# Linear attention and MLP layers on one core: the second value product in the sums' banks, a query product ahead of the first broadcasts, row statistics on ScalarE with spread transposes

## The chip, the cores and the metric

One Trainium2 chip, one of its cores. The metric is device time in microseconds (us) of one execution of the whole kernel; lower is better. PE is the matrix engine (TensorE), ACT the scalar engine, DVE the vector engine, POOL the GpSimd engine, SP the engine that issues the DMA transfers here. Each engine works through its own instructions in order and waits for the others by semaphores.

## What is computed

Four residual layers run one after the other on 2048 rows of 576 features in bfloat16: linear attention (A), MLP (B), and both again with the same weights. There are 32 heads of 18 features; the MLP is 4608 wide.

```python
def _A_ref(x, wqkv, wo):
    qkv = (x @ wqkv).reshape(B, S, 3, H, Dh).transpose(2, 0, 3, 1, 4)
    q, k, v = qkv[0], qkv[1], qkv[2]
    phi = lambda t: jnp.where(t > 0, t + 1, jnp.exp(t)) + 1e-6
    pq, pk = phi(q), phi(k)
    kv = jnp.einsum("bhsd,bhse->bhde", pk, v)
    z = jnp.einsum("bhsd->bhd", pk)
    num = jnp.einsum("bhqd,bhde->bhqe", pq, kv)
    den = jnp.einsum("bhqd,bhd->bhq", pq, z)[..., None] + 1e-6
    return (num / den).transpose(0, 2, 1, 3).reshape(B, S, D) @ wo

def _B_ref(x, w1, b1, w2, b2):
    h = _gelu(_layernorm(x) @ w1 + b1)
    return h @ w2 + b2

x = x + _A_ref(_layernorm(x), wqkv, wo)
x = x + _B_ref(_layernorm(x), w1, b1, w2, b2)
x = x + _A_ref(_layernorm(x), wqkv, wo)
x = x + _B_ref(_layernorm(x), w1, b1, w2, b2)
```

## The kernel before

**Tiling.** The rows are 16 tiles of 128 (t), or 4 blocks of 512 (c). The 32 heads form 5 groups (g) of 7, 7, 7, 7 and 4 heads, so 126 or 72 columns. The normalized rows stand turned in `yT`, features on partitions.

**PSUM.** There are eight banks. `ps_h` has four one-bank buffers in rotation, which serve key and query products, transposes (`tp`), denominators and broadcasts. `ps_acc` has two buffers of two banks, accA and accB. During the keys of an A layer accA holds `kvacc`, the running sums of keys times values, and accB every value product `v_ps`.

**LayerNorm pipe.** `LNPipe` carries tiles through stages, one per `tick`: statistics (L296 to L309, DVE), the reciprocal root by a power on POOL (L315), `ln_nmr` (L319), the norm into one of three `y_ring` buffers (L330 on POOL, L334 on DVE), and in the last stage five transposes on PE (L352) and a copy into `yT` (L354). `l0_norm_eng` (L759) gives the engine of the norm in the first layer. Other rows are turned through DRAM (`turn_rows`, `land`) and do not use PE.

**A layer, keys.** For each tile t: key product (`k_proj`, 10 matmuls, L449), a tick of the LayerNorm pipe, value product in two halves (`v_proj`, L462 and L470, copied to `v_ring` by ACT and DVE), the sums of the tile before (`kv_acc`, L488), and from some tile on one query product (`q_proj`, L494). In the first layer's opening the first value product is copied out by three ACT copies, one of them between its halves (L464 to L478). `phi` takes an exponent (L388) and a shift (L389) on ACT and two steps on DVE.

**A layer, passage.** The sums are masked (`kvT`, L518), the denominators of blocks 0 and 1 are formed and inverted (`den_stage` L556 to L564), spread (`quad_stage`, L569) and broadcast to the heads' columns by a matmul (`scale_stage`, L578), copied by ACT (L580) and multiplied into `pq` by DVE (L581). Five products `kvwo` (L540) alternate between accB and accA; odd ones are copied out by DVE (L545), even ones by ACT (L547). Four query products are woven in between.

**A layer, output.** `wo_stage` for each tile: ten matmuls (L589) into accA or accB in turn, the residual sum on DVE (L427), a store to DRAM. Between them stand the broadcasts of the next block, in the first layer the last query products, the denominators of blocks 2 and 3, and one tick of the LayerNorm pipe per tile, through which the first four tiles of the MLP (its first block) go. Each of these four is fed after its sum with `hold=1`, statistics on DVE, norm on POOL, transposes on PE, copy on ACT.

**MLP.** For each block 36 slices of the first product with GELU on ACT (L690 to L699), then the second product (L744).

PE's instructions have the order of the program text (`pe` chains them); the order on the other engines is that of a scheduler, held by the manual dependences in the text.

Of the kernel before, what the change touches and what calls it, by code (L numbers as in the profile page):

```python
# [34 lines left out]
def build(tc, A_x, A_wqkv, A_wo, B_w1, B_b1, B_w2, B_b2, out, dbg=None, n_layers=4):  # L35
    nc = tc.nc
    dbg = dbg or {}
    with ExitStack() as ctx:
# [182 lines left out]
        state = dict(ycnt=0, vcnt=0, turns=0)  # L221
# [42 lines left out]
        class LNPipe:  # L264
# [3 lines left out]
            def feed(self, xt, t, kind, norm_eng, evac_eng="dve", load_from=None, after=None, hold=0):  # L268
                self.items.append(dict(stage=(0 if load_from is None else -1), xt=xt, t=t, kind=kind,
                                       norm=norm_eng, evac=evac_eng, load=load_from,  # L270
                                       after=after, hold=hold))
# [4 lines left out]
            def tick(self, transposes=1):  # L276
                land()
                for it in list(self.items):
                    st = it["stage"]
                    if st == 4 and it["evac"] != "dma":  # L280
                        if transposes == 0:
                            continue
                        transposes -= 1
# [3 lines left out]
                    if st == -1:  # L287
# [4 lines left out]
                        it["xt"] = xn  # L292
                    elif st == 0:
# [23 lines left out]
                    elif st == 2 and it["norm"] != "dve":  # L317
                        nmr = work.tile([P, 1], F32, name="ln_nmr", bufs=4)
                        nc.gpsimd.tensor_scalar(out=nmr[:], in0=it["mv"][:, 0:1], scalar1=-1.0,  # L319
                                                scalar2=it["rstd"][:, 0:1], op0=ALU.mult, op1=ALU.mult)  # L320
                        it["nmr"] = nmr
                    elif st in (2, 3):
                        y = y_ring[state["ycnt"] % NY]
# [18 lines left out]
                    elif st == 4:  # L342
# [10 lines left out]
                        if it["evac"] == "act":  # L353
                            nc.scalar.copy(out=yT[:, :, t * P:(t + 1) * P], in_=tp)  # L354
                        else:
                            nc.vector.tensor_copy(out=yT[:, :, t * P:(t + 1) * P], in_=tp)
# [80 lines left out]
        def layer_A(li, next_kind, pre_a1=None):  # L437
            kvacc = ps_acc.tile([P, 2, 512], F32, name="kvacc", tag="accA")
# [17 lines left out]
            def v_proj(t):  # L456
# [3 lines left out]
                vp = ps_acc.tile([P, 2, 512], F32, name="v_ps", tag="accB")  # L460
# [3 lines left out]
                begin = li == 0 and t == 0  # L464
                if begin:
                    early = nc.scalar.copy(out=va[:, 0:2, 0:126], in_=vp[:, 0, 0:252].rearrange("p (g c) -> p g c", g=2))
                    for keys in ("exp", "phi"):
                        tc.add_manual_dep(early.ins, act_last[keys], NOSYNC, reason="keys before values")
                for k in range(KD):
                    pe(nc.tensor.matmul(vp[:, 1, 0:324], lhsT=yT[:, k, tok], rhs=wqkv_sb[:, k, 2 * D + 252: 3 * D],  # L470
                                     start=(k == 0), stop=(k == KD - 1)))
                if begin:
                    nc.scalar.copy(out=va[:, 2:4, 0:126], in_=vp[:, 1, 0:252].rearrange("p (g c) -> p g c", g=2))
                else:
                    nc.scalar.copy(out=va[:, 0:4, 0:126].rearrange("p (b g) c -> p b g c", b=2),
                                   in_=vp[:, :, 0:252].rearrange("p b (g c) -> p b g c", g=2))
                if begin:
# [5 lines left out]
            def kv_acc(t):  # L483
                pk = pk_tiles.pop(t)
                va = v_tiles.pop(t)
                for g in range(G):
# [30 lines left out]

            nc.vector.tensor_tensor(  # L518
# [65 lines left out]
            def wo_stage(t):  # L584
# [8 lines left out]
                if xn is not None and next_kind == "B" and t < TPC:  # L593
                    lnp.feed(xn, t, "B", "pool", "act", after="sum", hold=1)
# [22 lines left out]
            for t in range(NT):  # L617
# [141 lines left out]
        def l0_norm_eng(t):  # L759
            return "dve" if t < 2 else "pool"  # L760
# [99 lines left out]
```

## Time and profile before

| | us |
|---|---|
| median of three runs | 777.58 (777.58 to 777.61) |
| the profiled execution | 777.09 |
| its span, first to last instruction | 775.4 |
| PE busy in it | 765.1 |
| ACT busy | 335.1 |
| DVE busy | 277.7 |
| POOL busy | 120.5 |

The profile is one execution. A row of its timeline gives the start in us from the span's beginning, the length, the engine, the line, the operation with output and inputs, and how many were merged (x5); in brackets stands the time for which the engine had nothing to do before, and what ended it. A matmul's length reaches to its modelled end, later than the start of the next. Groups (`x144 | 91.2, 684 | ...`) give the count, the busy time in us, and the mean length in ns.

| stretch | us |
|---|---|
| keys of the first A layer | 7 to 67 |
| its passage | 67 to 80.5 |
| its output stage | 80.5 to 110 |
| first MLP | 110 to 395 |
| keys of the second A layer up to 449, passage | 449 to 461 |
| its output stage | 461 to 490 |
| second MLP | 490 to 775.4 |

### The profile page before, as it was taken

What the parts mean: (1) busy time and instruction counts of PE and PEld (TensorE: products, weight loads), DVE (VectorE), ACT (ScalarE), POOL (GpSimd) and SP (SyncE); (2) the same over time, 40 slices, a digit from 0 to 9 for tenths busy, and PEclk for the clock granted to TensorE, in tenths of its full rate; (3) what the DMA queues carried; (4) which work ended last, traced back from release to release, by engine and by line L of the source; (5) the groups of instructions that cost most, each with busy time, mean ns of one, the idle gap of its engine ahead of it and who ended that gap; (6) DMA issues with size and microseconds to landing.
All of it is one profiled execution on the core that took longest, in us unless ns stands there. A gap on an engine that the chain in (4) does not pass through costs nothing.

```text
span 775.4 us, 15774 instructions
## 1 busy us (share of the span) xinstructions
PE 765.1 (99%) x6613; PEld 495.0 (64%) x6613; DVE 277.7 (36%) x714; ACT 335.1 (43%) x734; POOL 120.5 (16%) x185
## 2 busy tenths in 40 slices
PE   8999999999999999999999999999999999999998
PEld 5776664675477457646777766547745764675476
DVE  7786964046013503401355579520140032000000
ACT  5888646404610650264046675561065026305600
POOL 4671322012000301200100004110030011001000
PEclk9999999999999999999999999999999999999999
DMA  8991474016301810320440006630141033011000
GB/s 254 267 299 46 137 253 103 18 50 173 88 16 48 199 50 32 92 64 17 138 107 1 1 2 210 248 82 8 32 129 52 16 124 80 8 32 54 1 11 21
DMA packets 73761, 69.10 MB, mean 89 GB/s; under 512 B 34266, under 2 KB 58330, under 8 KB 73690
## 3 DMA queue, kind: packets, MB, share of 16 engines
q1 hardware_dynamic: 73690, 68.10, 30.0%
q8 instruction: 51, 0.84, 0.5%
q14 instruction: 20, 0.16, 0.1%
HBM read 45.67 MB, written 22.41 MB: 88 GB/s over the span
## 4 chain that ended last, share of the span: by engine, by line
PE 94%; DVE 4%; issue 1%; ACT 1%; DMA 0%; POOL 0%; DVEq 0%; ACTq 0%
PE m_ps L744 37%; PE h_ps L694 20%; PE hp_ps L694 16%; PE q_ps L494 5%; PE k_ps L449 5%; PE wo_ps L589 4%; PE v_ps L470 3%; PE v_ps L462 2%; PE kvacc L488 1%; PE tp L352 1%; PE rden_ps L578 1%; PE warm_ps L176 1%; DVE rden L564 1%; DVE xo L427 0%; DMA x_d<-xo 0%
## 5 line engine op out<-in xcount | busy, mean ns | idle before, releaser
L744 PE MATMUL m_ps<-w_sb,hT 128*128 128x288 bf16 x2304 | 283.6, 286 | 0.0
L744 PEld LDWEIGHTS <-hT 128*128 128x128 bf16 x2304 | 224.8, 98 | 59.8 <-issue 3.4
L694 PEld LDWEIGHTS <-w_sb 64*128 64x128 bf16 x2304 | 124.5, 94 | 136.5 <-issue 1.9
L694 PE MATMUL hp_ps<-yT,w_sb 64*128 64x512 bf16 x1152 | 178.0, 376 | 0.0
L694 PE MATMUL h_ps<-yT,w_sb 64*128 64x512 bf16 x1152 | 148.0, 376 | 0.0
L699 ACT COPY relay_sb<-relay_sb 128x1 f32<-128x1 f32 x144 | 28.6, 198 | 264.5 <-PE h_ps L694 222.2
L315 POOL TENSOR_TENSOR ln_rstd<-ln_u,neg_half 128x1 f32<-128x1 f32 x64 | 36.8, 577 | 480.4 <-DVE ln_u L306 239.7
L690 ACT ACTIVATE hT<-h_ps,b1T 128x512 bf16<-128x512 f32 x144 | 91.2, 684 | 44.4 <-PE h_ps L694 44.4
L690 ACT ACTIVATE hT<-hp_ps,b1T 128x512 bf16<-128x512 f32 x144 | 91.2, 693 | 0.0
L427 DVE TENSOR_TENSOR xbf<-m_ps,xo 128x576 bf16<-128x576 f32 (+1 forms) x17 | 12.2, 722 | 219.9 <-PE m_ps L744 219.9
L427 DVE TENSOR_TENSOR xo<-m_ps,xo 128x576 f32<-128x576 f32 x16 | 12.1, 758 | 179.2 <-PE m_ps L744 179.2
L411 POOL TENSOR_TENSOR xo<-xo,b_bc 128x576 f32<-128x576 f32 x32 | 40.9, 1284 | 102.5 <-DMA xo<-x_d 62.7
L694 PE MATMUL h_ps<-yT,w_tail 64*128 64x512 bf16 x144 | 54.1, 376 | 0.0
L694 PE MATMUL hp_ps<-yT,w_tail 64*128 64x512 bf16 x144 | 54.1, 376 | 0.0
L494 PE MATMUL q_ps<-yT,wqkv_sb 128*126 128x512 bf16 (+1 forms) x200 | 50.0, 382 | 0.0
L589 PE MATMUL wo_ps<-kvwo,pq 126*128 126x288 bf16 (+1 forms) x320 | 43.9, 285 | 1.7 <-DVE pq L581 0.7
L449 PE MATMUL k_ps<-wqkv_sb,yT 128*128 128x288 bf16 x320 | 44.3, 286 | 0.0
L589 PEld LDWEIGHTS <-pq 126*128 126x128 bf16 (+1 forms) x320 | 30.2, 97 | 13.1 <-DVE pq L581 1.8
L449 PEld LDWEIGHTS <-yT 128*128 128x128 bf16 x320 | 31.0, 98 | 11.4
L694 PEld LDWEIGHTS <-w_tail 64*128 64x128 bf16 x288 | 27.1, 94 | 17.1
L388 ACT ACTIVATE phi_e<-k_ps 128x288 bf16<-128x288 f32 x46 | 19.3, 419 | 34.6 <-PE k_ps L449 33.6
L391 DVE TENSOR_SCALAR phi_e<-phi_e 128x288 bf16<-128x288 bf16 (+2 forms) x86 | 25.1, 292 | 24.6 <-ACT phi_e L388 24.5
(100 smaller groups left out, 633.2 us busy)
## 6 DMA issues: line engine op xcount, KB each, us to landing
xo<-x_d SPq DMA_DIRECT2D x48, 288.0 KB, 3.6
x_d<-xo SPq DMA_DIRECT2D x32, 288.0 KB, 2.1
xl<-x_d SPq DMA_DIRECT2D x24, 288.0 KB, 4.6
y_d<-turned SPq DMA_DIRECT2D x40, 144.0 KB, 3.2
w_sb<-in_B_w_dram SPq DMA_DIRECT2D x6, 864.0 KB, 9.5
yT<-y_d SPq DMA_DIRECT2D x10, 512.0 KB, 4.1
w_sb<-in_B_w_dram SPq DMA_DIRECT2D x9, 512.0 KB, 5.6
x_d<-xn SPq DMA_DIRECT2D x16, 288.0 KB, 2.2
```

The lines of the kernel that those rows point to most:

```text
L315: nc.gpsimd.tensor_tensor(out=rstd[:], in0=it["u"][:], in1=neg_half[:], op=ALU.pow)
L391: nc.vector.tensor_scalar(out=e[0:rows, 0:n], in0=e[0:rows, 0:n], scalar1=1.0, scalar2=1e-6, op0=ALU.min, op1=ALU.add)
L411: nc.gpsimd.tensor_tensor(out=xo[:], in0=xo[:], in1=b2_bc[:], op=ALU.add)
L427: total = nc.vector.tensor_tensor(out=xn[:, cols].rearrange("p (h n) -> p h n", h=nh), in0=ps, in1=xo[:, cols].rearrange("p (h n) -> p h n ...
L449: pe(nc.tensor.matmul(kp[:, 0:HALF], lhsT=yT[:, k, tok], rhs=wqkv_sb[:, k, D + half * HALF: D + (half + 1) * HALF], start=(k == 0), stop=( ...
L470: pe(nc.tensor.matmul(vp[:, 1, 0:324], lhsT=yT[:, k, tok], rhs=wqkv_sb[:, k, 2 * D + 252: 3 * D], start=(k == 0), stop=(k == KD - 1)))
L494: pe(nc.tensor.matmul(qp[0:GR[g], :], lhsT=wqkv_sb[:, k, GO[g]:GO[g] + GR[g]], rhs=yT[:, k, c * CA:(c + 1) * CA], start=(k == 0), stop=(k ...
L589: pe(nc.tensor.matmul(wp[:, half, 0:HALF], lhsT=pq[(g, c)][0:GR[g], j * P:(j + 1) * P], rhs=kvwo[g][0:GR[g], half * HALF:(half + 1) * HALF ...
L690: act_last["gelu"] = nc.scalar.activation(out=to, in_=ps, func=ACT.Gelu_apprx_tanh, bias=b1T[:, f:f + 1], scale=1.0).ins.name
L694: mm = pe(nc.tensor.matmul(dst[n], lhsT=wt, rhs=mv, start=(seen[n] == 0), stop=(seen[n] == 8)))
L699: relay = nc.scalar.copy(out=relay_sb[:, 1:2], in_=relay_sb[:, 0:1])
L744: pe(nc.tensor.matmul(acc[:, half, 0:HALF], lhsT=hT[f][:, j * P:(j + 1) * P], rhs=w2_sb[:, f, half * HALF:(half + 1) * HALF], start=(f == ...
```

## The change

It has three parts. First, in the first layer the value product of tile 1 goes into accA and `kvacc` is allocated only with the first sums; the sums of tile 0 move behind the key product of tile 2; the three ACT copies of value product 0 become one of ACT and one of DVE, and value product 1 takes the ACT copies; tile 3's norm moves from POOL to DVE. Second, in the passage of both A layers one query product moves from between `kvwo` 2 and 3 to before the first broadcasts. Third, for the four tiles that an A layer hands to the MLP, the statistics are made by two passes on ACT (an Identity with scale -1/D that sums to the negative mean, and a Square with that as its bias that sums to the variance times D), with one small step on POOL for the variance plus epsilon; no more than three tiles may hold a `y_ring` buffer; a second tick without transposes is made per output tile up to t = 9; the transposes of tile t wait until output tile 6 + 2t.

```diff
-        state = dict(ycnt=0, vcnt=0, turns=0)
+        state = dict(wo=0, ycnt=0, vcnt=0, turns=0)
...
-            def feed(self, xt, t, kind, norm_eng, evac_eng="dve", load_from=None, after=None, hold=0):
+            def feed(self, xt, t, kind, norm_eng, evac_eng="dve", load_from=None, after=None, hold=0, stats="dve", tp_at=0):
...
-                        if transposes == 0:
+                        if transposes == 0 or state["wo"] < it["tp_at"]:
                             continue
...
+                    elif st == 0 and it["stats"] == "act":
+                        mv = it["mv"] = work.tile([P, 2], F32, name="ln_mv", bufs=6)
+                        it["dump"] = blk.tile([P, D], BF16, name="ln_dump", tag="blk")
+                        nc.scalar.activation(out=it["dump"][:], in_=it["xt"][:, 0:D], func=ACT.Identity,
+                                             scale=-1.0 / D, accum_out=mv[:, 0:1])
+                        it["stage"] = 0.5
+                        continue
+                    elif st == 0.5:
+                        u = it["u"] = work.tile([P, 1], F32, name="ln_u", bufs=4)
+                        mv = it["mv"]
+                        nc.scalar.activation(out=it.pop("dump")[:], in_=it["xt"][:, 0:D], func=ACT.Square,
+                                             bias=mv[:, 0:1], accum_out=mv[:, 1:2])
+                        nc.gpsimd.tensor_scalar(out=u[:], in0=mv[:, 1:2], scalar1=(1.0 + EPS) / D, scalar2=EPS * EPS,
+                                                op0=ALU.mult, op1=ALU.add)
+                        it["stage"] = 1
+                        continue
...
+                        if sum(other["stage"] == 4 for other in self.items) == NY:
+                            continue
...
-                            nc.scalar.copy(out=yT[:, :, t * P:(t + 1) * P], in_=tp)
+                            turned_tile = nc.scalar.copy(out=yT[:, :, t * P:(t + 1) * P], in_=tp)
+                            if act_last["exp"] is not None:
+                                tc.add_manual_dep(turned_tile.ins, act_last["exp"], NOSYNC, reason="keys go on first")
...
-            kvacc = ps_acc.tile([P, 2, 512], F32, name="kvacc", tag="accA")
+            kvacc_of = {}
...
-                vp = ps_acc.tile([P, 2, 512], F32, name="v_ps", tag="accB")
+                begin = li == 0 and t < 2
+                vp = ps_acc.tile([P, 2, 512], F32, name="v_ps", tag="accA" if begin and t == 1 else "accB")
...
+                copy = nc.scalar.copy(out=va[:, 0:4, 0:126].rearrange("p (b g) c -> p b g c", b=2),
+                                      in_=vp[:, :, 0:252].rearrange("p b (g c) -> p b g c", g=2))
                 if begin:
...
+                    for keys in ("exp", "phi"):
+                        tc.add_manual_dep(copy.ins, act_last[keys], NOSYNC, reason="keys before values")
+                if begin and t == 1:
                     nc.scalar.copy(out=va[:, 4, 0:72], in_=vp[:, 1, 252:324])
                 else:
                     nc.vector.tensor_copy(out=va[:, 4, 0:72], in_=vp[:, 1, 252:324])
...
+                if t == 0:
+                    kvacc_of["ps"] = ps_acc.tile([P, 2, 512], F32, name="kvacc", tag="accA")
+                kvacc = kvacc_of["ps"]
...
+                if li == 0 and t == 2:
+                    kv_acc(0)
                 pre_a1(t)
                 v_proj(t)
-                if t >= 1:
+                if t >= (2 if li == 0 else 1):
                     kv_acc(t - 1)
...
-                    lnp.feed(xn, t, "B", "pool", "act", after="sum", hold=1)
+                    lnp.feed(xn, t, "B", "pool", "act", hold=1, stats="act", tp_at=6 + 2 * t)
...
             q_proj(*q_left.pop(0))
             kv_wo(1)
+            q_proj(*q_left.pop(0))
             for g in range(3):
                 scale_stage(g, 0)
             kv_wo(2)
-            q_proj(*q_left.pop(0))
             kv_wo(3)
...
+                state["wo"] = t
                 lnp.tick()
+                if t < 10:
+                    lnp.tick(transposes=0)
...
-            return "dve" if t < 2 else "pool"
+            return "pool" if t == 2 or t > 3 else "dve"
```

More of the change, by code (lines that the diff above doesn't have):

```diff
@@ L318, in tick @@
                         nmr = work.tile([P, 1], F32, name="ln_nmr", bufs=4)
-                        nc.gpsimd.tensor_scalar(out=nmr[:], in0=it["mv"][:, 0:1], scalar1=-1.0,
+                        nc.gpsimd.tensor_scalar(out=nmr[:], in0=it["mv"][:, 0:1], scalar1=1.0 if it["stats"] == "act" else -1.0,
                                                 scalar2=it["rstd"][:, 0:1], op0=ALU.mult, op1=ALU.mult)
@@ L463, in v_proj @@
                                      start=(k == 0), stop=(k == KD - 1)))
[L464 to L468, printed above, removed]
                 for k in range(KD):
@@ L516, in layer_A @@
             q_proj(*q_left.pop(0))
+            kvacc = kvacc_of["ps"]
             nc.vector.tensor_tensor(
```

7 lines of the change are left out of this document (1 added, 6 removed).

## The prediction

> **What bounds the kernel now.** I read the page's busy times first, then the busy time by stage, then the list of waits, and last the order of time around each wait.
>
> ```profile
> span 775.4 us, 15774 instructions
> PE 765.1 (99%) x6613; PEld 495.0 (64%) x6613; DVE 277.7 (36%) x714; ACT 335.1 (43%) x734; POOL 120.5 (16%) x185
> ```
>
> TensorE (PE) sets the end. The change neither adds nor removes a matmul, so all it can move is PE's idle time, 775.4 - 765.1 = 10.3 us by the record. The stages say where that lies:
>
> ```profile
> 7.00:15.00 8.00, 7.09 (x65) 5.50 (x63) 5.71 (x21) 5.03 (x14) 3.86 (x7) 1.00 1.06 335
> 15.00:67.00 52.00, 52.00 (x456) 40.36 (x455) 39.40 (x133) 42.70 (x104) 32.67 (x57) 1.00 0.86 246
> 67.00:80.50 13.50, 12.61 (x117) 7.92 (x116) 10.45 (x30) 11.13 (x23) 0.00 (x0) 1.00 0.01 1
> 80.50:110.00 29.50, 28.53 (x257) 19.66 (x258) 25.03 (x60) 15.79 (x28) 9.53 (x16) 1.00 0.56 192
> 449.00:461.00 12.00, 11.30 (x112) 7.10 (x109) 9.08 (x26) 9.72 (x19) 0.00 (x0) 1.00 0.00 0
> 461.00:490.00 29.00, 27.21 (x249) 18.62 (x249) 24.43 (x57) 14.58 (x26) 9.32 (x16) 1.00 0.59 200
> ```
>
> The columns are stretch, length, then PE, weight loads, DVE, ACT, POOL. PE idles 0.91 us in the opening, 0.89 and 0.70 us in the two passages from keys to the output stage, 0.97 and 1.79 us in the two output stages: 5.26 us, and all three parts of the change lie there. In the output stages DVE is the fullest of the other engines (25.03 of 29.5 us), ACT half empty. The granted clock is 1.00 in all of them. The record hides some idle time: a matmul's row runs on after the next could have started, so each stop loses about 0.16 us more than it shows (in the rows below, 0.70 against 0.54 from start to start).
>
> Two lines of the list of waits (waiting, waited for, us in total, times, longest) that the rows further down do not show:
>
> ```profile
> PE rden_ps L578 <- DVE rden L564: 0.8, 2, 0.4
> ...
> PE tp L352 <- POOL y_ring L330: 0.4, 1, 0.4
> ```
>
> **Part 1, the second value product in accA (gain 1.25 us).** The PE rows of the opening are: first half and second half of value product 0, transposes of tile 2, value product 1, sums 0, key product 2; the others are the steps that part 1 leans on.
>
> ```profile
> 4.79 1.07 POOL L315 TENSOR_TENSOR ln_rstd<-ln_u,neg_half 128x1 f32<-128x1 f32 x2 [2.49 <-DVE ln_u L306]
> ...
> 5.38 0.94 DVE L334 TENSOR_SCALAR y_ring<-x,ln_mv,ln_rstd 128x576 bf16<-128x576 bf16 x2 [0.30 <-POOL ln_rstd L315]
> ...
> 9.74 0.70 PE L462 MATMUL v_ps<-wqkv_sb,yT 128*128 128x252 bf16 x5
> ...
> 11.06 0.85 PE L470 MATMUL v_ps<-wqkv_sb,yT 128*128 128x324 bf16 x5 [0.61 <-ACT v_ring L466]
> ...
> 11.74 0.44 PE L352 MATMUL tp<-ident,y_ring 128*128 128x128 bf16 x5
> ...
> 12.32 0.71 ACT L354 COPY yT<-tp 128x640 bf16<-128x640 bf16 x1
> 12.48 0.70 PE L462 MATMUL v_ps<-wqkv_sb,yT 128*128 128x252 bf16 x5 [0.30 <-ACT v_ring L478]
> ...
> 12.52 0.15 DVE L306 TENSOR_SCALAR ln_u<-ln_mv 128x1 f32<-128x1 f32 x1
> ...
> 13.02 0.85 PE L470 MATMUL v_ps<-wqkv_sb,yT 128*128 128x324 bf16 x5
> ...
> 13.71 0.42 PE L488 MATMUL kvacc<-pk,v_ring 128*128 128x126 bf16 x5
> ...
> 13.90 0.58 ACT L475 CAST v_ring<-v_ps 128x504 bf16<-128x504 f32 x1 [0.88 <-PE v_ps L470]
> ...
> 13.97 1.39 PE L449 MATMUL k_ps<-wqkv_sb,yT 128*128 128x288 bf16 x10
> ```
>
> From start to start an unhindered first half takes 13.02 - 12.48 = 0.54 us, a second half 13.71 - 13.02 = 0.69, the five sums 0.26, and five transposes some 0.27 (an estimate: their row of 0.44 less the hidden end of 0.16). The early copy between the halves of product 0 goes, and product 1 gets banks of its own, so both waits lose their cause. From 9.74: 10.28, 10.97, 11.24 (transposes), 11.78, 12.47, with the five sums, now behind key product 2, 12.73 in all against 13.97. That is 1.24, call it 1.25: 0.91 shown and two hidden ends. What is late next: key product 2 at 12.47 needs tile 2 in yT. ACT copies value 0 (0.58 us) from about 11.16, then yT (0.71) until 12.4, which just fits. Sums 0 must wait until accA is copied out; the key product's 1.23 us hide that. Tile 3's transposes now come at 13.97. Its statistics end at 12.67, POOL's power (0.55 us, half of the first row) at 13.4, and its norm, now on DVE (0.47, half of the second), at 13.9: that fits by a hair too. Bounds: 0.6 us if those two miss by 0.3 each, 1.25 if they fit. Behind it PE has no gap from 15 to 67 us, DVE and ACT are about 80% busy, and the later norms have room, so the gain should last.
>
> **Part 2, a query product ahead of the first broadcasts (loss 0.1 us twice).** It should cover the two stops of 0.3 and 0.4 us in front of and between the broadcasts. But ACT takes its work in order, and the query's two exponent passes now stand ahead of the three copies.
>
> ```profile
> 74.90 0.41 PE L540 MATMUL kvwo_ps<-wo_sb,kvT 126*126 126x288 bf16 x2
> ...
> 75.59 0.59 ACT L389 ACTIVATE phi_a<-q_ps 126x512 bf16<-126x512 f32 x1
> 75.62 0.59 PE L578 MATMUL rden_ps<-quad_rden,head_bc 128*128 128x512 bf16 x2 [0.31 <-DVE quad_rden L569]
> 76.07 1.57 ACT L580 CAST rden_bc<-rden_ps 126x512 bf16<-126x512 f32 x3
> ...
> 77.05 1.24 PE L494 MATMUL q_ps<-yT,wqkv_sb 128*126 128x512 bf16 x5
> 77.26 0.75 DVE L545 CAST kvwo<-kvwo_ps 126x576 bf16<-126x576 f32 x1
> 77.49 0.69 ACT L547 CAST kvwo<-kvwo_ps 126x576 bf16<-126x576 f32 x1
> ...
> 80.59 1.58 PE L589 MATMUL wo_ps<-kvwo,pq 126*128 126x288 bf16 x10 [0.29 <-DVE kvwo L545]
> ```
>
> The query runs 75.14 to 76.23 (row ends 76.38). The second broadcast still waits for the second reciprocal (76.58). ACT, free at 76.08, waits for the query until 76.41, spends two steps of about 0.49, and begins the copies at 77.4 instead of 76.07; its copy of kvwo 2 ends at 79.5 instead of 78.18. On PE kvwo 3 wants accA, which DVE frees at 78.01, unmoved: a wait of 0.8 us from 77.25, which the query used to fill. kvwo 4 wants accB from that ACT copy: at 79.55, another 0.8 us. The last query then ends at 80.9, and the first output product starts there, 0.3 later than 80.59, but without its inner wait of 0.2: 0.1 lost. The second A stage has the same rows 381.5 us later. Bounds: gain 0.7 each if the queue on ACT proves slack, loss 0.5 each.
>
> **Part 3, statistics on ACT and spread transposes (gain 1.2 and 1.6 us).** Here the place and not the amount decides. The first row is one half of a tile's statistics on DVE, in the first output stage.
>
> ```profile
> L296 DVE BATCH_NORM_STATS2 ln_st<-xn 128x6 f32<-128x288 f32 x4 | 1.8, 438 | 0.0
> ```
>
> DVE sheds two such passes for each of four tiles, 8 x 0.44 = 3.5 us per stage, and the two short steps behind each pair. ACT gains eight passes over 576 columns. None is in the trace; the nearest row is the 576-column copy (0.69). A per-partition bias adds 0.09 by the rows below (GELU with one, 684, against 0.59 for phi_a). I take 0.69 and 0.78; the lower end is 0.59 (phi_a's 512 columns), the upper 0.69 + 0.09 + 0.20, a small instruction more for the sum along the row.
>
> ```profile
> L699 ACT COPY relay_sb<-relay_sb 128x1 f32<-128x1 f32 x144 | 28.6, 198 | 264.5 <-PE h_ps L694 222.2
> L690 ACT ACTIVATE hT<-h_ps,b1T 128x512 bf16<-128x512 f32 x144 | 91.2, 684 | 44.4 <-PE h_ps L694 44.4
> ```
>
> "VectorE: DVE Perf Modes" of the Trainium skill, section on two Vector instructions with no wait between them, counts an operation that also writes out its accumulator as two instructions; it says so of VectorE, and no row here shows it for ScalarE. If it held there each pass would be 0.2 longer; by that the sum below would be 2.9 us and not 4.05. What follows does without it.
>
> ```profile
> 91.33 0.37 DVE L569 TENSOR_TENSOR quad_rden<-quad_mask,rden 128x512 bf16<-128x512 bf16 x1
> ...
> 91.76 0.61 PE L578 MATMUL rden_ps<-quad_rden,head_bc 128*128 128x512 bf16 x2 [0.85 <-DVE ln_u L309]
> ...
> 99.32 0.61 PE L578 MATMUL rden_ps<-quad_rden,head_bc 128*128 128x512 bf16 x2
> ...
> 109.68 1.04 PE L694 MATMUL h_ps<-yT,w_sb 64*128 64x512 bf16 x8
> ...
> 469.36 0.65 PE L589 MATMUL wo_ps<-kvwo,pq 126*128 126x288 bf16 x4 [0.37 <-DVE xo L427]
> ...
> 470.52 0.91 PE L589 MATMUL wo_ps<-kvwo,pq 72*128 72x288 bf16 x6 [0.51 <-DVE pq L581]
> ...
> 489.87 1.04 PE L694 MATMUL h_ps<-yT,w_sb 64*128 64x512 bf16 x8
> ```
>
> First output stage: the broadcasts of block 2 wait for its spread denominators, behind two rows of statistics on DVE. Without those the reciprocal and sum 3 follow directly, the spread ends at 91.05 and the broadcast starts at 91.1 and not 91.76, the 0.1 of part 2 included. The transposes of tiles 1 to 3 then no longer crowd ahead of block 3: only tile 0's has been done when its broadcast starts, at 97.9 by the same steps; the old one started at 99.32 with 0.55 us more transposes behind it, so 0.85 ahead. The transposes left come at output tiles 8, 10 and 12, when their norms are long done, so the stop for POOL's norm goes too. Stage end 108.5 against 109.68: 1.2 us net of part 2's 0.1, so 1.3 alone. ACT's in-order queue is the cover: four tiles of passes take 5.9 us, its idle share is 13.7 us, and the first copy of block 2 stays at 91.9.
>
> Second stage: output tile 4 still stops, since the scale of the last group now stands behind sum 3: until 470.1 and not 470.52, so 0.4. All later stops (1.4 with their hidden ends) shrink to about 0.2: 488.2 against 489.87, 1.6 us net, 1.7 alone. POOL takes over one small step per tile; SP's reloads of residual rows, which wait for the norms, come earlier, with the stores queued behind them.
>
> **Sum.** 1.25 - 0.1 - 0.1 + 1.3 + 1.7 = 4.05; for the slips that a schedule on paper misses I take 3.5. The profiled execution's own time was 777.09, its span 775.4: 773.6. The median of the runs lies 0.49 above it, at 777.58: **774.1**.
>
> **Rivals.** *A longer row pass (slower).* With 1.3 us per pass instead of 0.7 ACT holds back block 1's last copy and all of block 2's; the first copy of block 2 then ends at 96.6, the broadcast slots and transposes behind it come late, and block 3's broadcast starts at 102.2. The same steps give the first stage 3.0 us over its old end, the second 1.7; less 1.1 from part 1: 781.2. It decides from about 1.0 us per pass. Against it: every 576-column row is under 0.75. *The queries pay too.* If ACT's order matters less, the 0.7 us in each passage is saved: 774.1 - 0.7 - 0.7 - 0.2 = 772.5. The full ACT (10 us busy of 12) speaks against it. *The waits only move.* If the sums take the place of the statistics in front of reciprocal and scale, the output stages keep their time and only part 1 is left, with 1.0: 776.6. For it: sums are 12 of DVE's 25 us and stand ahead of both.
>
> **How the numbers follow.** Forecast 0.57, queries 0.11, waits only move 0.16, longer pass 0.16. The forecast's own range: 0.6 us from the opening, and 0.5 from each passage, give 775.0; all of the paper sum and 0.5 more give 773. Down to the queries' case and up towards the third: 772.6 to 776.9. A measurement of this kernel tells about 0.2% from no change, 1.56 us, so faster begins below 776.0: forecast, queries and a third of the case of moved waits, 0.73; the same: the rest of that case and the mildest of the fourth, 0.13; slower 0.14.
>
> **What would show it.** Key product 2 starting near 12.5 us, sums 0 behind it. In the passage two waits of 0.8 us, for DVE and ACT, at kvwo 3 and 4. Row passes of 0.7 to 0.8 us. The first broadcast of block 2 near 91.1 less the 1.2 of the opening, so 89.9. It is wrong if passes last 1 us, if key product 2 waits for ACT's copy, or if PE's idle time in the two output stages stays at 0.97 and 1.79.

## The result and the profile after

The changed kernel takes 775.14 us (median of 8 runs, 775.0 to 775.75), the kernel before in the same set 777.6 (777.15 to 778.07): a ratio of 0.997, 95% interval 0.9961 to 0.9979. The gain is clear of the spread of the runs, but it is 2.5 us by the medians, where 3.5 had been forecast. The profiled execution took 775.0 us. Its page begins:

```profile
span 773.3 us, 15768 instructions
...
PE 763.3 (99%) x6607; PEld 495.2 (64%) x6613; DVE 272.4 (35%) x683; ACT 345.9 (45%) x765; POOL 118.7 (15%) x191
```

The busy time by stage, with the same columns as before:

```profile
7.00:15.00 8.00, 8.00 (x78) 6.55 (x76) 6.41 (x26) 6.38 (x17) 2.54 (x5) 1.00 1.08 340
...
67.00:80.50 13.50, 12.20 (x114) 7.69 (x113) 10.39 (x29) 11.15 (x22) 0.00 (x0) 1.00 0.01 1
80.50:110.00 29.50, 28.74 (x263) 19.68 (x266) 22.00 (x41) 20.19 (x43) 9.79 (x20) 1.00 0.62 205
449.00:461.00 12.00, 10.71 (x104) 6.61 (x103) 10.01 (x27) 10.46 (x20) 0.00 (x0) 1.00 0.00 0
461.00:490.00 29.00, 27.74 (x263) 19.34 (x266) 20.99 (x38) 19.16 (x41) 9.03 (x20) 1.00 0.65 219
```

The opening has no PE idle time left. By the record the two passages idle more than before (1.30 and 1.29 us against 0.89 and 0.70). The two output stages idle 0.76 and 1.26 us against 0.97 and 1.79, although DVE was relieved there by 3.0 and 3.4 us, as planned, and ACT took 4.4 and 4.6 us more.

For a ledger, fixed windows don't do, since everything shifts, and the profile lacks a few matmul records. What is comparable is the start of the same PE row in each kernel. Five marks serve: the first key product, `z_ps` (the first product from the masked sums), the first output product, the one-row matmuls (`eps_row`) that end the denominators of block 2, and the first MLP product. Time is counted from the first key product, because the start-up ahead of it differs from one execution to the next: in the profiled executions of this study that product starts anywhere from 7.25 to 8.09 us, in kernels that differ only behind it. In us from mark to mark:

| | first key product | to `z_ps` | to output product | to block 2's denominators | to MLP | to `z_ps`, layer 2 | to output product | to denominators | to MLP | to the end | total |
|---|---|---|---|---|---|---|---|---|---|---|---|
| before | 7.29 | 63.89 | 9.41 | 7.51 | 21.58 | 342.97 | 9.41 | 3.91 | 23.90 | 285.53 | 768.11 |
| after | 7.31 | 62.65 | 9.70 | 7.33 | 21.26 | 342.97 | 9.70 | 3.72 | 23.18 | 285.48 | 765.99 |
| difference | | -1.24 | +0.29 | -0.18 | -0.32 | 0 | +0.29 | -0.19 | -0.72 | -0.05 | -2.12 |

The opening gives 1.24 us (forecast 1.25), each passage costs 0.11 and 0.10 (forecast 0.1), and the two output stages, columns "to MLP", give 0.32 and 0.72 where 1.3 and 1.7 had been forecast. All that is missing is missing in part 3. (The ledger compares one execution of each kernel; its 2.12 us and the 2.46 of the medians differ by 0.34 that is not located.)

**The opening as drawn.** PE rows of the changed kernel:

```profile
9.76 0.70 PE L483 MATMUL v_ps<-wqkv_sb,yT 128*128 128x252 bf16 x5
10.29 0.85 PE L486 MATMUL v_ps<-wqkv_sb,yT 128*128 128x324 bf16 x5
...
12.48 1.39 PE L469 MATMUL k_ps<-wqkv_sb,yT 128*128 128x288 bf16 x10
13.71 0.42 PE L507 MATMUL kvacc<-pk,v_ring 128*128 128x126 bf16 x5
13.97 0.44 PE L370 MATMUL tp<-ident,y_ring 128*128 128x128 bf16 x5
```

Key product 2 starts at 12.48 (forecast 12.47), the sums follow it, and the transposes of tile 3 start at 13.97, where the hair's breadth held. No PE row of the opening has a wait.

It held in this execution; it doesn't hold in all. Eight of the experiments below share this opening with the same stretch to `z_ps`, 62.65 to 62.70 us, but e6 and e10 need 62.84, e2 62.86 and e7 63.17, though their edits lie elsewhere. In e6 the sums start at 13.71 as above, but the transposes of tile 3 at 14.14, 0.17 late. In e7 the rows of tile 2 arrive late (its statistics start at 7.96 instead of 6.85), and PE waits for POOL's norm:

```profile
11.52 0.45 PE L370 MATMUL tp<-ident,y_ring 128*128 128x128 bf16 x5 [0.35 <-POOL y_ring L348]
```

So the opening gives 0.72 to 1.24 us, counted against the one profiled execution of before. Below, stages are compared one by one, since the totals carry this too.

**The passage as drawn.** ACT and PE rows of the first layer:

```profile
75.20 0.60 ACT L408 ACTIVATE phi_e<-q_ps 126x512 bf16<-126x512 f32 x1 [0.24 <-PE q_ps L513]
...
76.17 1.57 ACT L602 CAST rden_bc<-rden_ps 126x512 bf16<-126x512 f32 x3
...
76.84 0.41 PE L562 MATMUL kvwo_ps<-wo_sb,kvT 126*126 126x288 bf16 x2 [0.64 <-DVE kvwo L567]
...
78.34 0.40 PE L562 MATMUL kvwo_ps<-wo_sb,kvT 72*72 72x288 bf16 x2 [0.66 <-ACT kvwo L569]
```

The three broadcast copies (L602) stand behind the exponent passes of the moved query, and the two predicted waits are there: `kvwo` 3 for DVE, `kvwo` 4 for ACT, 0.64 and 0.66 by the record, 0.8 with the hidden end of 0.16. The old stops are gone. The gap is the output stages.

### The profile page after: what moved, and what is told of

Its sections match the earlier page's. It is cut to its first block, busy times and chain, and to the rows that moved or that the text cites. A ratio compares the mean times of both kernels' runs of the same rounds, so it can differ in the third digit from the quotient of the medians.

```text
span 773.3 us, 15768 instructions
## 1 busy us (share of the span) xinstructions
PE 763.3 (99%) x6607; PEld 495.2 (64%) x6613; DVE 272.4 (35%) x683; ACT 345.9 (45%) x765; POOL 118.7 (15%) x191
## 4 chain that ended last, share of the span: by engine, by line
PE 94%; DVE 2%; ACT 1%; DMA 1%; POOL 1%; issue 1%; DVEq 0%; POOLq 0%; ACTq 0%
PE m_ps L769 37%; PE h_ps L719 20%; PE hp_ps L719 16%; PE q_ps L513 6%; PE k_ps L469 5%; PE wo_ps L611 3%; PE v_ps L486 3%; PE v_ps L483 2%; PE kvacc L507 1%; PE tp L370 1%; ACT rden_bc L602 1%; PE rden_ps L600 0%; DMA xo<-x_d 0%; DVE xo L447 0%; DMA x<-in_A_x_dram 0%
```

## The experiments

Each kernel is measured by the same marks; "after" stands for the changed kernel. Ratios are against the kernel before, with their 95% intervals.

**The parts by themselves.** e1_opening keeps part 1 and takes parts 2 and 3 back.

```diff
-                    lnp.feed(xn, t, "B", "pool", "act", hold=1, stats="act", tp_at=6 + 2 * t)
+                    lnp.feed(xn, t, "B", "pool", "act", after="sum", hold=1)
...
             kv_wo(1)
-            q_proj(*q_left.pop(0))
...
             kv_wo(2)
+            q_proj(*q_left.pop(0))
...
                 lnp.tick()
-                if t < 10:
-                    lnp.tick(transposes=0)
```

> Only part 1 (second value product in accA, sums 0 behind key product 2, tile 3's norm on DVE). Theory: the opening's gain is 1.23 us and is carried to the end, so span 774.2 us, and the two passages and output stages last what they lasted before (first broadcast of the first output stage to the first MLP matmul as before). Rival: some of the gain is given back where a later stage waits for something that does not move with PE: span 774.7 to 775.4.

Median 776.18 us, ratio 0.9986 (0.9976 to 0.9995). Total from the first key product 766.88: the opening 62.65 as in after, every other stretch within 0.02 of before (9.41, 7.51, 21.59; 9.41, 3.91, 23.89). The opening's gain is carried to the end whole, which was the theory (a span of 774.2 had been expected, 774.3 came).

e2_q_back takes back part 2 alone (the two moved `q_proj` lines above).

> The changed kernel without part 2 (the query product back between kvwo 2 and 3). Theory: part 2 costs 0.1 us in each passage and nothing else, so span 773.1 (773.3 less 0.2); the two waits of 0.64 us for kvwo copies are gone and the ones for spread and reciprocal (0.3 and 0.4) are back. Rival: the other order of ACT's queue helps the output stage, so taking it away costs: span 773.6 or more.

Median 774.57, ratio 0.9968 (0.9956 to 0.998), total 765.61. The passages fall back to 9.41 with 7.52 and 3.91 behind them, 0.10 less each than in after. The second output stage is 0.43 shorter too (22.75 against 23.18), which no term of the prediction had; neither did the expectation of 0.1 us each "and nothing else", and its rival, that the new order helps the output stage, has it the wrong way round. The scheduler's order on ACT differs behind the passage as well: in e2 the copies of block 1 at 465.02 stand ahead of tile 0's Square pass, in after (at 465.13) such copies stand behind it. That this costs the 0.43 is possible, but no run shows it by itself. The total holds 0.21 us more of the opening than after's.

e2 against e1 is part 3 without part 2: 0.34 us in the first output stage (21.59 to 21.25) and 1.14 in the second (23.89 to 22.75).

**The two halves of part 3.** e3_dve_stats keeps the spread transposes and puts the statistics back on DVE; e4_early_tp keeps the statistics on ACT and lets the transposes come when they will.

```diff
# e3_dve_stats
-                    lnp.feed(xn, t, "B", "pool", "act", hold=1, stats="act", tp_at=6 + 2 * t)
+                    lnp.feed(xn, t, "B", "pool", "act", after="sum", hold=1, tp_at=6 + 2 * t)
# e4_early_tp
-                    lnp.feed(xn, t, "B", "pool", "act", hold=1, stats="act", tp_at=6 + 2 * t)
+                    lnp.feed(xn, t, "B", "pool", "act", hold=1, stats="act")
```

> The changed kernel with the four tiles' statistics on DVE again; the spread transposes and the second tick stay. Theory A: taking the statistics off DVE earned the output stages' 0.32 and 0.72 us, so they are lost: span 774.3, block 2's first broadcast waits about 0.7 longer. Theory B: the spread transposes earned it, and ACT's passes (0.69 and 0.78 us and two accumulator reads of 0.2) give back what they free on DVE: span 773.3 or below.

> The changed kernel with statistics on ACT but the transposes as soon as a tile's turn comes (tp_at 0). Theory A (statistics earn it): span within 0.2 of 773.3. Theory B (spread transposes earn it): PE meets the POOL norms again, stops of 0.4 us or more in front of transposes, span 774.0 to 774.5.

e3: median 775.95, ratio 0.9984 (0.9975 to 0.9993), total 766.75, output stages 21.72 and 23.42. e4: median 778.14, ratio 1.0012 (1.0002 to 1.0021), total 768.79, stages 23.20 and 23.99. So, with part 2 and the second tick in place, the spread transposes without the moved statistics cost 0.14 in the first stage (21.58 before) and give 0.48 in the second, and the moved statistics without the spread transposes lengthen both, by 1.62 and 0.09. Neither theory fits as written: e3 loses 0.46 and 0.24 against after where theory A had all of the 0.32 and 0.72, and e4 comes out beyond even theory B's 774.5 (a span of 776.7). Why shows in the PE rows of e4's first output stage:

```profile
92.38 0.53 PE L370 MATMUL tp<-ident,y_ring 128*128 128x128 bf16 x5 [0.71 <-POOL y_ring L348]
...
94.93 0.40 PE L370 MATMUL tp<-ident,y_ring 128*128 128x128 bf16 x4 [0.35 <-POOL y_ring L348]
```

With the statistics early, the transposes stand in PE's order right behind POOL's norms, and PE waits for those. The spread transposes are what makes the moved statistics pay; each is worth more with the other.

**What a row pass costs.** The groups of the changed kernel's passes on ACT in the first output stage (count, busy us, mean ns):

```profile
L303 ACT ACTIVATE ln_dump<-xn,ln_mv 128x576 bf16<-128x576 f32 x4 | 3.1, 786 | 0.0
L296 ACT ACTIVATE ln_dump<-xn 128x576 bf16<-128x576 f32 x4 | 2.8, 689 | 0.1
...
L296 ACT ACTIVATION_READ_ACCUMULATOR ln_dump<-xn 128x1 f32 x4 | 0.8, 203 | 0.0
```

The passes last 0.69 and 0.79 us, the prices taken; but behind each stands a second instruction of 0.20 that reads out the sum. To see what it adds, starts are compared:

```profile
83.58 0.69 ACT L296 ACTIVATE ln_dump<-xn 128x576 bf16<-128x576 f32 x1
...
84.15 0.20 ACT L296 ACTIVATION_READ_ACCUMULATOR ln_dump<-xn 128x1 f32 x1
84.25 1.07 ACT L602 CAST rden_bc<-rden_ps 126x512 bf16<-126x512 f32 x2
...
85.19 0.80 ACT L303 ACTIVATE ln_dump<-xn,ln_mv 128x576 bf16<-128x576 f32 x1
85.87 0.22 ACT L303 ACTIVATION_READ_ACCUMULATOR ln_dump<-xn,ln_mv 128x1 f32 x1
85.96 0.59 ACT L408 ACTIVATE phi_e<-q_ps 72x512 bf16<-72x512 f32 x1
```

The read begins before the pass's row ends, and the next instruction 0.10 and 0.09 behind the read's start: from 83.58 to 84.25 is 0.67, from 85.19 to 85.96 is 0.77, 1.44 us per tile with the reads, against the 1.47 of the prediction. (The 1.9 us per tile in some of the expectations further down adds the rows' lengths and is too much.) "VectorE: DVE Perf Modes" of the Trainium skill, section "Two Vector instructions with no wait between them", counts an operation that writes out its accumulator as two instructions; these rows show the second one on ScalarE as well, and that it takes 0.1 us of the engine and not the 0.2 of its row. So the price was right. What the length of a pass does to the end was tried from both sides.

e5_half_pass takes the statistics over the first 288 of the 576 columns only, so each pass is 0.24 us shorter (445 and 542 ns); e6_double_pass makes every pass twice.

```diff
# e5_half_pass
-                        nc.scalar.activation(out=it["dump"][:], in_=it["xt"][:, 0:D], func=ACT.Identity,
-                                             scale=-1.0 / D, accum_out=mv[:, 0:1])
+                        nc.scalar.activation(out=it["dump"][:, 0:HALF], in_=it["xt"][:, 0:HALF], func=ACT.Identity,
+                                             scale=-1.0 / HALF, accum_out=mv[:, 0:1])
...
# e6_double_pass
+                        nc.scalar.activation(out=it["dump"][:], in_=it["xt"][:, 0:D], func=ACT.Identity,
+                                             scale=-1.0 / D, accum_out=mv[:, 0:1])
...
+                        nc.scalar.activation(out=dump[:], in_=it["xt"][:, 0:D], func=ACT.Square,
+                                             bias=mv[:, 0:1], accum_out=mv[:, 1:2])
```

> The changed kernel with the ScalarE statistics over 288 of the 576 columns (the other half of each row is left out), so each pass 0.24 us shorter, 1.9 us of ACT per stage; the scheduler also reorders ACT and DVE around them. Counted from the first key product (65.99 more precisely 765.99 us to the end in the changed kernel), stretches from the eps product of block 2's denominators to the first MLP matmul 21.26 and 23.18. Theory 1 (the passes were under-priced: 1.9 us per tile with the accumulator reads, not 1.47, and hold up the copies that reciprocal 3 waits behind): both stretches shrink by 0.4 or more, total gain 0.8 to 1.5. Theory 2 (POOL's norms stretch the spreads on DVE, 0.85 and 0.74 us instead of 0.39): both stretches stay within 0.2.

> The changed kernel with each of the eight ScalarE passes per stage done twice (same result), so 3.8 us of ACT per tile instead of 1.9. My slower rival, a longer row pass, says that this turns the gain into a loss: first output stage at least 3 us longer, second at least 1.7, total from the first key product 769 or more against 768.1 before the change. If ACT's queue has the room that I gave it: each stage under 1 us longer.

e5: median 774.15, ratio 0.9965 (0.9947 to 0.9982), total 765.09, stages 20.96 and 22.57, so 0.30 and 0.61 shorter than after: near theory 1, which had 0.4 or more for both, and outside the 0.2 of theory 2. e6: median 785.14, ratio 1.0098 (1.0075 to 1.0121), total 774.89, stages 25.05 and 28.08, so 3.8 and 4.9 longer. The end hangs on ACT in the output stages. In e6 (its lines stand five further down), where the first copies of block 2 start at 96.03, the chain is plain:

```profile
95.27 0.78 ACT L308 ACTIVATE ln_dump<-xn,ln_mv 128x576 bf16<-128x576 f32 x1
...
96.03 1.06 ACT L607 CAST rden_bc<-rden_ps 126x512 bf16<-126x512 f32 x2
...
96.66 0.38 PE L605 MATMUL rden_ps<-quad_rden,head_bc 128*128 128x512 bf16 x1 [1.47 <-ACT rden_bc L607]
```

Passes stand in front of the broadcast copies, and PE waits for a copy to free the bank of the next broadcast. That is the mechanism of the rival "a longer row pass", in the place that it named: it had the first copy of block 2 end at 96.6.

**Where the changed kernel loses it.** By the record the first output stage has a single stop of PE, at block 3's broadcast. The steps that lead to it, on all engines:

```profile
90.07 0.61 PE L600 MATMUL rden_ps<-quad_rden,head_bc 128*128 128x512 bf16 x2
...
91.16 1.05 ACT L602 CAST rden_bc<-rden_ps 126x512 bf16<-126x512 f32 x2
...
92.10 0.78 ACT L303 ACTIVATE ln_dump<-xn,ln_mv 128x576 bf16<-128x576 f32 x1
...
92.87 1.54 ACT L602 CAST rden_bc<-rden_ps 126x512 bf16<-126x512 f32 x3
...
95.20 0.94 DVE L586 RECIPROCAL rden<-den_ps 128x128 bf16<-128x128 f32 x1
...
96.07 0.69 DVE L447 TENSOR_TENSOR xn<-wo_ps,xo_pair 128x576 f32<-128x576 f32 x1
96.44 0.82 POOL L348 TENSOR_SCALAR y_ring<-xn,ln_rstd,ln_nmr 128x576 bf16<-128x576 f32 x1
96.68 0.85 DVE L591 TENSOR_TENSOR quad_rden<-quad_mask,rden 128x512 bf16<-128x512 bf16 x1
...
97.59 0.61 PE L600 MATMUL rden_ps<-quad_rden,head_bc 128*128 128x512 bf16 x2 [0.49 <-DVE quad_rden L591]
```

The first broadcasts of block 2 come 0.58 us earlier than in e1 (90.07 against 90.65, with block 2's denominators at 86.99 in both), but their copies don't (91.16 against 91.08): in after, a Square pass of 0.76 us that began at 90.40 stands in front of them. At the copies, what DVE's relief had won is gone. The last Square pass (92.10) holds back the next copies; DVE idles 0.30 us for one at 93.48 and then has no gap up to the reciprocal. This reading of the rows has no run of its own. Then, on DVE, the sum of tile 7 goes ahead of the spread, and the spread lasts 0.85 us instead of 0.41, beside a POOL norm. The sum and the spread have runs of their own. e8_spread_first drops the dependence that ties the spread behind the sum; e7_spread_psum writes the reciprocal to PSUM (there in float32, not rounded to bfloat16), so that the spread has one SBUF input instead of two.

```diff
# e8_spread_first
-                    quad_stage(late, after=dve_last["sum"])
+                    quad_stage(late)
# e7_spread_psum
-                rden = work.tile([P, P], BF16, name="rden", bufs=1)
...
-                    nc.vector.reciprocal(out=rden[:], in_=dp[:, 0:P])
+                rden = dp[:, P:2 * P]
+                nc.vector.reciprocal(out=rden, in_=dp[:, 0:P])
```

> The changed kernel without the order 'sums first' for the spreads of blocks 2 and 3; only one pair of DVE instructions changes places, sum 7 and spread 3 in the first A layer. If block 3's broadcast is late because reciprocal, sum and spread stand in one row on DVE, the stop of 0.49 us there goes and the first output stage is 0.4 to 0.65 shorter (21.26 to about 20.7), the second unchanged at 23.18. If ACT is what is late, the stage stays within 0.1.

> The changed kernel with the reciprocal of the denominators written to PSUM in float32, so that the spread on DVE reads one operand from SBUF and not two. The spread then lasts about 0.6 (512 columns from PSUM). Theory 2 (POOL's norm blocks a DVE operation with two SBUF operands): no spread over 0.65 us any more, the stretch before block 3's broadcast 0.2 to 0.3 shorter in the first output stage, in the second the wait for the last group's scale 0.1 to 0.3 shorter. Theory 1: the spreads were not what was late, stretches within 0.1 or 0.2 longer for the slower spread.

e8: median 774.84, ratio 0.9967 (0.9952 to 0.9981), total 765.40: the first output stage 20.59 against 21.26, no other stretch by more than 0.02. e7: median 775.88, ratio 0.9979 (0.9968 to 0.9991), total 766.86. DVE and POOL rows of e7:

```profile
468.11 0.82 POOL L348 TENSOR_SCALAR y_ring<-xo,ln_rstd,ln_nmr 128x576 bf16<-128x576 f32 x1
468.46 0.68 DVE L590 TENSOR_TENSOR quad_rden<-quad_mask,den_ps 128x512 bf16<-128x512 bf16 x1
...
475.88 0.68 DVE L590 TENSOR_TENSOR quad_rden<-quad_mask,den_ps 128x512 bf16<-128x512 bf16 x1
476.17 0.82 POOL L348 TENSOR_SCALAR y_ring<-xo,ln_rstd,ln_nmr 128x576 bf16<-128x576 f32 x1
```

From PSUM the spread lasts 0.68 us whether a norm was running when it began (first pair) or not (second pair), so the stretching is gone. But 0.68 is more than the 0.41 of an unhindered spread: the second output stage gains 0.34 (22.84), while the first loses 0.28 and each stretch to block 2's denominators 0.19 or 0.20: in these four stretches 0.33 is lost. Another 0.52 of the 0.87 by which its total exceeds after's is the late opening shown above. Theory 2 had the mechanism, but its limit of 0.65 for a spread is missed by 0.03, and its gain of 0.2 to 0.3 in the first stage is a loss.

**Do the savings add?** e9_both joins e2 and e8. e10_late_stats also holds the statistics of tiles 2 and 3 back by four ticks (`hold=5 if t >= 2 else 1`); e11_late_only is e2 with that hold alone.

> The changed kernel with two edits undone or turned: the query product back between kvwo 2 and 3 (as in e2_q_back), and the spread ahead of the sum in the late blocks (as in e8_spread_first). Counted from the first key product, the changed kernel takes 765.99 us, e2 765.61, e8 765.40. If the two losses are separate (one is ACT's queue in the passage and behind it, the other DVE's order in the first output stage), the savings add: 765.0, with 9.41 us from keys to first output product in both layers, 20.6 us from block 2's denominators to the MLP in the first output stage and 22.75 in the second. If both come out of one and the same lateness of block 2 on ACT, they overlap: 765.4, with one of the two stages no shorter than in the better of e2 and e8. Median 774.0 by the first, 774.5 by the second.

> e9_both, with the statistics of the MLP's tiles 2 and 3 held back by four more ticks, so that their ACT passes (1.9 us per tile with the read of the accumulator) no longer stand in ACT's queue before or between the copies of block 2's broadcasts. If what is left of the lateness in the output stages is ACT's queue, block 2's copies start up to 1.9 us earlier per tile moved and the two stages together shrink by another 0.3 to 0.8 us from e9. If the copies wait for PE's broadcasts, and those for DVE's reciprocals, the stages keep their time within 0.1 us, or lengthen where the later norms hold up the transposes of output tiles 10 and 12.

> As e10_late_stats, but with the sum ahead of the spread as in the changed kernel. If the late statistics act by relieving ACT, and the order on DVE acts by itself, this run differs from e2_q_back in the output stages by the same amount by which e10 differs from e9, and from e10 by the 0.67 us of the first output stage. If the delay of block 3's broadcast came only from ACT's passes having pushed the reciprocal behind the sum, the late statistics alone bring the first output stage from 21.25 to 20.6 us, and e10 is no better than this run.

e9: median 774.35, ratio 0.996 (0.9948 to 0.9973), total 765.17, stages 21.25 and 22.58. That looks like the second theory, but the run doesn't bear on the first stage: there DVE still does the sum first (96.38, the spread at 96.99 for 0.85), since dropping a dependence only allows the other order. e10: 774.91, ratio 0.9969 (0.9957 to 0.9981), total 765.81, stages 20.68 and 23.63. e11: 775.31, ratio 0.9973 (0.9962 to 0.9983), total 766.01, stages 20.92 and 23.63. Both predictions about late statistics fail in part: the first stage gains 0.57 and 0.33 against e9 and e2, but the second loses 1.05 and 0.88. The 0.67 expected between e10 and e11 in the first stage is 0.24. In e9 the passes of tiles 2 and 3 stand ahead of the first copies of block 2; held back, one pair stands ahead of block 2's last copy (with a copy into `yT` between), which delays output tile 8. Rows of e10:

```profile
473.82 0.78 ACT L303 ACTIVATE ln_dump<-xo,ln_mv 128x576 bf16<-128x576 f32 x1
...
475.16 0.58 ACT L602 CAST rden_bc<-rden_ps 72x512 bf16<-72x512 f32 x1
...
476.25 0.91 PE L611 MATMUL wo_ps<-kvwo,pq 72*128 72x288 bf16 x6 [0.89 <-DVE pq L603]
```

In e10 the scheduler also put the spread of block 3 first (96.19), so that its first stage mixes two causes; e11, with the sum first, is the clean one.

e12_forced is e9 with the sum of tile 7 tied behind the spread; nothing else in the order of the engines' instructions differs from e9.

```diff
+                for late in list(rden_of) if (li, t) == (0, 7) else (): quad_stage(late)
                 wo_stage(t)
...
-                dve_last["sum"] = total.ins.name
+                dve_last["sum"] = total.ins.name; li == 0 and t >= 7 and tc.add_manual_dep(total.ins, dve_last["spread"], NOSYNC, reason="spread first")
```

> e9_both asked for the spread of block 3 ahead of the sum of tile 7 by dropping a dependence, and its DVE rows show the sum first all the same (96.38, spread at 96.99 for 0.85 us), so it could not tell whether the savings add. Here the sum of tile 7 in the first A layer is tied behind the spread; nothing else in the order of any engine differs from e9. If the savings are separate, the first output stage falls from 21.25 us (e9) to the 20.6 of e8, and the others stay at e9's, passages 9.41, second output stage 22.58: 764.5 us from the first key product, median 773.7. If block 3's broadcast, half a us earlier, only moves the wait to another place in the stage, it stays at 21.2 and the total at 765.2.

Median 773.64 us (5 runs, 773.49 to 774.35), ratio 0.9956 (0.9943 to 0.997), total 764.55 (764.5 expected), stages 20.59 and 22.58: the savings add. Rows of e12 that answer to those of after:

```profile
95.03 0.94 DVE L586 RECIPROCAL rden<-den_ps 128x128 bf16<-128x128 f32 x1
96.01 0.43 DVE L591 TENSOR_TENSOR quad_rden<-quad_mask,rden 128x512 bf16<-128x512 bf16 x1
96.27 0.87 POOL L348 TENSOR_SCALAR y_ring<-xn,ln_rstd,ln_nmr 128x576 bf16<-128x576 f32 x1
...
96.77 0.60 PE L600 MATMUL rden_ps<-quad_rden,head_bc 128*128 128x512 bf16 x2
```

The spread, now ahead of the norm as well as of the sum, lasts 0.43 us, PE no longer waits, and it is POOL's norm that is a little longer (0.87 against 0.82). This version is faster than the kernel before. Against the changed kernel its ledger is 1.44 us shorter and its slowest run is below the fastest of after (775.0), but the two were timed in different sets, and the intervals of their ratios touch (up to 0.997, and from 0.9961).

## Why the prediction held in direction and missed in size

- **Part 1** was right in mechanism and size: 1.24 against 1.25, with the sums behind key product 2 at the predicted time, and e1 shows it alone. Both things that "fit by a hair" fitted in that execution, and that is partly luck: in e2, e6 and e10 tile 3's transposes come about 0.2 us late, and in e7 those of tile 2 wait for a norm, which no bound of the prediction had. Its lower bound of 0.6 was no idle caution.
- **Part 2** was right: 0.11 and 0.10 lost, two waits at the named instructions. "The queries pay too" fell with that. What the prediction didn't see is that the same edit costs another 0.43 us in the second output stage (e2) and, with the spread untied as well, 0.60 (e9 against after).
- **Part 3** is the step that failed in size: 1.3 and 1.7 forecast, 0.32 and 0.72 measured (0.34 and 1.14 without part 2). Its first link held: block 2's first broadcast starts at 90.07 (forecast 89.9). The price of the passes held too (1.44 against 1.47 us per tile; the reads add 0.1 and not the 0.2 of its side estimate, whose sum of 2.9 us is not worked out there). Wrong was the sentence "ACT's in-order queue is the cover: four tiles of passes take 5.9 us, its idle share is 13.7 us". A share is an average. The passes come when a sum is done, and that is where the copies of the broadcasts are due. In the first stage the first copy of block 2 was to "stay at 91.9", so at 90.7 after the opening's gain; it came at 91.16, behind a Square pass. It shows best at output tile 4 of the second stage:

```profile
466.05 0.38 PE L600 MATMUL rden_ps<-quad_rden,head_bc 128*128 128x512 bf16 x1
466.07 0.69 ACT L296 ACTIVATE ln_dump<-xo 128x576 bf16<-128x576 f32 x1
...
466.89 0.78 ACT L303 ACTIVATE ln_dump<-xo,ln_mv 128x576 bf16<-128x576 f32 x1
...
467.66 0.56 ACT L602 CAST rden_bc<-rden_ps 72x512 bf16<-72x512 f32 x1
467.89 0.74 DVE L447 TENSOR_TENSOR xo<-wo_ps,xo 128x576 f32<-128x576 f32 x1
...
468.56 0.41 DVE L603 TENSOR_TENSOR pq<-pq,rden_bc 72x512 bf16<-72x512 bf16 x1
...
469.02 0.91 PE L611 MATMUL wo_ps<-kvwo,pq 72*128 72x288 bf16 x6 [0.87 <-DVE pq L603]
```

The last broadcast of block 1 is done at 466.43. Its copy waits for both passes of a tile and starts at 467.66; the scale on DVE then falls behind the next sum, and PE stops for 0.87 us. The prediction saw a stop here, for a DVE reason, and none for ACT. With halved passes the copy starts earlier and this stop is gone; what remains is 0.35 us for a sum, in the rows of e5:

```profile
466.41 0.56 ACT L602 CAST rden_bc<-rden_ps 72x512 bf16<-72x512 f32 x1
...
467.73 1.46 PE L611 MATMUL wo_ps<-kvwo,pq 126*128 126x288 bf16 x9 [0.35 <-DVE xo L447]
```

- **The order on DVE.** That "the reciprocal and sum 3 follow directly" was right for block 2, to within 0.2 us. For block 3 the prediction took "the same steps", but there the sum of tile 7 had its data when the reciprocal ended and went ahead of the spread, and the spread ran into a norm. Its broadcast came at 97.59, where 96.7 had been forecast (97.9 less the opening's 1.2). The swap of sum and spread is worth 0.66 us of the first stage (21.25 in e9, 20.59 in e12), and it is the rival "the waits only move" in a small way: a sum in front of the spread where statistics had stood.
- **The account.** Of the 3.0 us forecast for part 3, 1.04 came. The swap in the first stage is worth 0.66, the query's order with the untied spread 0.60 in the second. What is left, 0.7 us, stays open in e12; its one large stop is that at output tile 4 (0.81 us by the record), which e5 lays to the passes on ACT, though the scheduler placed other instructions differently in that run too.
- **"A longer row pass"** did not happen, but e6 shows that its lever was real: with the passes doubled the kernel is slower than before by 1.0%.

## What to carry to other kernels

Idle share doesn't make an in-order queue a cover: list what stands in the queue at the moment the new instructions become ready, and follow the one right behind them to who waits for it. When work leaves an engine, look at what moves up into its place; the order of two instructions on DVE was worth half of the gain planned for its stage. A step that fits by a hair on paper fits in some executions only. And untying a dependence gives the scheduler a choice, not the order that one wants, so the order has to be read from the build, or forced.

## What the runs showed of the hardware

- A pass on ACT that sums along the row is followed by an instruction of its own, 0.19 to 0.22 us long in its row, and ACT's next instruction starts 0.09 to 0.10 us behind the start of that one, where it doesn't need the sum (rows 84.15 and 85.87 of after).
- A spread on DVE (two SBUF inputs) that begins during a norm on POOL is stretched to the norm's end and 0.26 to 0.27 us beyond it. Three spreads of after did (0.85, 0.74 and 0.57 us; rows above: norm 96.44 to 97.26, spread to 97.53); begun ahead of the norm it lasted 0.43, and the norm 0.87 instead of 0.82 (e12). With one input from PSUM it lasted 0.68 in both orders (e7). That agrees with "SBUF — State Buffer" of the Trainium skill, section "Who interferes with whom": a DVE instruction with two SBUF inputs contends with a GpSimd instruction that reads SBUF, and one with at most one SBUF input doesn't, outside the 2-port perf modes.
- The first key product started between 7.25 and 8.09 us in executions of kernels that differ only behind it. That is as much as several of the effects above, which is why the ledger begins behind it. In e2, where it is latest, DVE waited 0.72 us for rows of x that were still under way (the second tile's statistics start at 4.56, in after at 3.79).
